# Pads that let the two operands of nearly all matrix products begin at one place modulo 512 bytes, and one shared temporary of the router

## The chip, the core and the metric

The kernel runs on one core of a Trainium2 chip. Its time is the device time of one execution in microseconds (us). The core's engines are TensorE (PE; its weight loads are a row of their own, PEld), VectorE (DVE), ScalarE (ACT), GpSimd (POOL) and SyncE (SP), which issues most DMAs. Each runs its own instructions in order and waits for others by semaphores.

## The reference: what is computed

Three layers follow each other: masked attention with decaying weights (4 sequences of 576 positions, 8 heads of 64), a dense mixture of 8 experts over the 2304 tokens, weighted by a matrix P that eight rounds of row and column normalisation make, and a mixture in which each token goes to one expert.

```python
# attention, per batch and head
ret = scale * (q @ k.T) * where(i >= j, gamma ** (i - j), 0);  x = ret @ v      # x: [2304, 512]
# dense mixture: E = 8, D = 512, F = 1024
P = exp(x @ w_gate - max);  8 times: rows of P to sum 1, columns of P to sum N / E
out = sum over e of P[:, e] * (relu(x @ w1[e]) @ w2[e])
# mixture with one expert per token
e = argmax(x @ w_gate);  out = softmax(x @ w_gate)[e] * (relu(x @ w1[e]) @ w2[e])
```

## The kernel before, in words

All products are done in a split form: an fp32 operand a is kept as a high part in the format fp32r and a low part (the rest), and a product becomes three matmuls: high by high, high by low, low by high. On TensorE a matmul is a weight load (the stationary operand, 128 columns of 4 bytes, so 512 bytes in each partition) and a matmul that streams the moving operand (512 columns, 2048 bytes, in most places) past it. A row `pyt<-w2hi,hhi` of the profile names the result, the moving operand and the stationary one, in that order.

The stages, in order of time:

- **Attention** (`attention`): 16 pairs of heads, in an order that a table of numbers (`TAU`) sets. Its matmuls are transposes (L160, 128 or 64 columns), scores (L209) and outputs (L273) of 256 or 128 columns, and small products of 128 columns (L235).
- **Dense mixture** (`Dense`), two sweeps of 16 units (half of an expert each). `hidden` makes the hidden rows of eight tiles of tokens by seven products of combined blocks, 84 matmuls of 512 columns in a unit (L608, in `product`): moving operands `op0h` to `op6l` of pool `xT`, stationary ones `w0h` to `w6l` of pool `b_w1`. `y_tile` (L730) multiplies 128 hidden rows by `w2hi`, `w2lo` in 12 matmuls of 512 columns; the hidden rows are stationary: `hhi`, `hlo` of pool `b_h`. In the first sweep two more tiles are made the plain way by `rest_hidden` (L705, 256 columns, moving `xrh`, `xrl`, stationary `w0h` to `w3l`), and their rows `rhi`, `rlo` of pool `b_r` are the stationary operands of 24 matmuls at L730. ACT and DVE split the next unit's weights beside it and evict the results.
- **Router** (`Router`): the choice of expert, beside the second sweep, in small DVE instructions.
- **Slots** (`Top1`): 22 slots of 128 tokens that share an expert were executed here. `hidden` (L1248, 24 matmuls of 512 columns, moving `op0h` to `op3l`, stationary `xth`, `xtl`), transposes (`th` L1260, `tx` L1227), `result` (L1276, 24 matmuls of 512 columns, moving `op4h` to `op6l` and `u7h`, `u7l`, stationary `hth`, `htl`). `split` (L1214 on ACT, L40 on DVE, or on POOL for the units 3 and 7) makes each expert's weights ready.

In ACT, DVE and PE the order of the code is the order of the instructions. In a slot, ACT has the queue hrow, hth, xth, hth, then the splits 0, 1, 3, 2 of the next slot, and then 4, 5; DVE has the low parts of the same.

A tile's place is fixed when the program is built: the tiles of a pool lie behind each other in the order in which they are made, each rounded up to 32 bytes, and a pool lies behind the one that was opened before it. The pools `b_h`, `b_q`, `b_w2`, `b_w1` and `xb` are laid from the other end (`side="right"`).

```python
for k in range(2):                                                    # product, around L608
    for ww, xx in ((wh, xh), (wl, xh), (wh, xl)):
        self.nc.tensor.matmul(bank, ww[:, k, 128 * p:128 * p + 128], xx[:, k, :], ...)
for hh, ww in ((hhi, vhi), (hhi, vlo), (hlo, vhi)):                   # y_tile, around L730
    nc.tensor.matmul(pt, hh, ww, start=n == 0, stop=n == 11)
mm = [(hi, fc, w[fc][i]) for fc in fcs for i in range(2)]             # result, around L1276
mm += [(lo, fc, w[fc][0]) for fc in fcs]
```

Of the kernel before, what the change touches and what calls it, by code (L numbers as in the profile page):

```python
# [10 lines left out]
F32 = mybir.dt.float32  # L11
# [12 lines left out]
E = 8  # L24
# [26 lines left out]
def attention(tc, ctx, q, k, v, gk, gq, ident, xseg, extra=(), npairs=16):  # L51
# [11 lines left out]
    const = ctx.enter_context(tc.tile_pool(name="a_const", bufs=1))  # L63
# [8 lines left out]
        return ENG[LO[k]]  # L72

    gk_sb = const.tile([128, H + 2 * NPAIR], F32, name="gk_sb")
    gq_sb = const.tile([128, NPAIR, 128], F32, name="gq_sb")
    kTs = [[const.tile([128, 640], F32R, name=f"kT{i}_{j}") for j in range(2)] for i in range(BUFS["kT"])]
    qbds = [[const.tile([128, 1152], F32R, name=f"qbd{i}_{j}") for j in range(2)] for i in range(BUFS["qbd"])]
# [307 lines left out]
class Pumped:  # L385


    def __init__(self, eng):
        self.eng, self.bg = eng, []
# [393 lines left out]
class Router:  # L783
# [8 lines left out]
    def __init__(self, tc, ctx, crow, ident, wg2, acc, x2d, res, pt):  # L792
        self.tc, self.nc, self.ident, self.acc, self.pt = tc, tc.nc, ident, acc, pt
        self.x2d, self.res = x2d, res
        nc = self.nc
        self.v = Pumped(nc.vector)
        self.pool = pool = ctx.enter_context(tc.tile_pool(name="r_sb", reuse_waits="tile", bufs=1))
        self.C = pool.tile([128, CKEEP], F32, name="crow")
        nc.scalar.dma_start(self.C, crow[:, 0:CKEEP])
        self.wg = pool.tile([128, KD, E], F32, name="wg2")  # L800
        nc.scalar.dma_start(self.wg, wg2.rearrange("(k p) e -> p k e", p=128))
        self.C16 = pool.tile([128, 3, 128], BF16, name="c16")
        with tc.tile_pool(name="r_c", reuse_waits="tile", bufs=1) as tmp:
            t = tmp.tile([128, 384], F32, name="crow_b")
            nc.scalar.dma_start(t, crow[:, CKEEP:CKEEP + 384])
            nc.vector.tensor_copy(self.C16.rearrange("p a b -> p (a b)"), t)
        self.L = pool.tile([128, NT, E], F32, name="L2")
        self.Bm = pool.tile([128, NT, 128], BF16, name="Bm")
        self.q = pool.tile([128, NT], F32, name="rq")
        self.gp = pool.tile([128, 3, NT], BF16, name="gparts")  # L810
        self.oh = [pool.tile([128, E, n], BF16, name=f"oh{n}") for n in (NEARLY, NLATE)]
        self.xt = pool.tile([128, KD, 128], F32, name="rxt")
        self.B = [{}, {}]

    def c(self, k):
# [17 lines left out]
    def choose(self, b, pool):  # L833

        nc, v = self.nc, self.v
        i0, n = ((0, NEARLY), (NEARLY, NLATE))[b]
        L = self.L[:, i0:i0 + n, :]
        m = pool.tile([128, n], F32, name=f"m{b}")
        eq = pool.tile([128, n, E], F32, name=f"eq{b}")
        mm = pool.tile([128, n], F32, name=f"mm{b}")  # L840
        w = self.c("w").unsqueeze(1).to_broadcast([128, n, E])
        v.tensor_reduce(out=m, in_=L, axis=AX.X, op=ALU.max)
        v.tensor_tensor(out=eq, in0=L, in1=m.unsqueeze(2).to_broadcast([128, n, E]), op=ALU.is_equal)
        v.tensor_tensor(out=eq, in0=eq, in1=w, op=ALU.mult)
        v.tensor_reduce(out=mm, in_=eq, axis=AX.X, op=ALU.max)
        v.tensor_tensor(
            out=self.oh[b].rearrange("p e i -> p i e"), in0=w,
            in1=mm.unsqueeze(2).to_broadcast([128, n, E]), op=ALU.is_equal,
        )
        self.B[b].update(m=m, i0=i0, n=n, pool=pool)  # L850

    def count(self, b):
        nc, r = self.nc, self.B[b]
# [116 lines left out]
    def early(self, pool):  # L970

        nc, v = self.nc, self.v
        n = NEARLY
        sel = pool.tile([128, E, n], F32, name="s0_sel")
        a = pool.tile([128, n], F32, name="s0_a")
        at = pool.tile([128, 2, n], F32, name="s0_at")
        z = pool.tile([128, n, 2, 2], BF16, name="s0_z")
        v.tensor_tensor(
            out=sel, in0=self.oh[0], in1=self.st.unsqueeze(2).to_broadcast([128, E, n]), op=ALU.mult
        )  # L980
        v.tensor_reduce(out=a, in_=sel.rearrange("p e i -> p i e"), axis=AX.X, op=ALU.add)
        for t in range(2):
            v.scalar_tensor_tensor(
                out=at[:, t, :], in0=self.q[:, 0:n], scalar=float(t), in1=a, op0=ALU.is_equal,
                op1=ALU.mult,
            )
        for t in range(2):
            v.tensor_scalar(
                out=z[:, :, 0, t], in0=at[:, t, :], scalar1=self.c("p"), scalar2=None, op0=ALU.mult
            )  # L990
            v.tensor_tensor(out=z[:, :, 1, t], in0=at[:, t, :], in1=self.c("i")[:, 0:n], op=ALU.mult)
        self.z0 = z
# [341 lines left out]
def build(ctx, tc, q, k, v, moe_w_gate, moe_w1, moe_w2, moe2_w_gate, moe2_w1, moe2_w2,  # L1334
          c_gk, c_gq, c_row, out):
    nc = tc.nc
    const = ctx.enter_context(tc.tile_pool(name="const", bufs=1))
    dram = ctx.enter_context(tc.tile_pool(name="dram", bufs=1, space=bass.MemoryType.DRAM))
    x2d = dram.tile([N, DM], F32, name="x2d")
    xbd = dram.tile([128, (NBLK - PB0) * KD * 64], F32, name="xbd")  # L1340
    ident = const.tile([128, 128], F32, name="ident")
    make_identity(nc, ident)
    res = {
        "gidx0": const.tile([128, 2], U32, name="gidx0"),
# [46 lines left out]
    with ExitStack() as cx:  # L1391
        lgp = cx.enter_context(tc.tile_pool(name="lgT", bufs=1, side="right"))
        xbp = cx.enter_context(tc.tile_pool(name="xb", bufs=1, side="right"))
        xb = xbp.tile([128, NBLK - PB0, KD, 64], F32, name="xb")

        def xseg(b, n):
            m = min(max(PB0 - b, 0), n)
            return ([(xa, b, m)] if m else []) + ([(xb, b + m - PB0, n - m)] if m < n else [])

        with ExitStack() as c2:  # L1400
            nc.scalar.dma_start(wg, moe_w_gate.rearrange("(k p) e -> p k e", p=128))
            p = nc.gpsimd
            tasks = token_tasks(nc, xa[:, 0:16], ops, [p, p, p, p, p, p, p])
            extra = [(4.0, lambda _: D.load1(0)), (5.0, lambda _: D.load2(0)),
                     (8.3, lambda ps: gate(ps, "ps", xa, 0, 4, 0)),
                     (8.5, lambda ps: gate(ps, "ps", xa, 4, 4, 8)),
                     (11.8, lambda ps: gate(ps, "ps", xa, 8, 2, 16))]
            extra += [(8.8 + 0.5 * i, lambda _, t=t: t()) for i, t in enumerate(tasks)]
            with tc.manual_schedule(engines={mybir.EngineType.SP}):
                attention(tc, c2, q, k, v, c_gk, c_gq, ident, xseg, extra)  # L1410
        aux = ctx.enter_context(tc.tile_pool(name="aux", reuse_waits="tile", bufs=1, space=PSUM))
        D.pt = aux
        for i in range(0, NT - NEARLY, 4):
            gate(aux, "rt", xb, NEARLY + i, 4, 2 * i)
        nc.sync.dma_start(xbd, xb.rearrange("p b k t -> p (b k t)"))
# [143 lines left out]
    with tc.manual_schedule(engines=MANUAL):  # L1559
# [58 lines left out]
    n = nc.values_load(  # L1618
        res["nslot"][0:1, 0:1], min_val=NFULL, max_val=NSLOT,
        skip_runtime_bounds_check_because="18 to 26 slots hold 2304 tokens of 8 experts",  # L1620
    )
# [40 lines left out]
```

## Time and profile before

| | |
|---|---|
| time of 3 runs: median (lowest to highest) | 2022.6 us (2021.27 to 2023.38) |
| time of the profiled execution | 2022.26 us |
| its span, from the first to the last instruction | 2020.5 us |
| busy: PE, PEld, DVE, ACT, POOL | 1981.2, 1630.0, 1251.7, 847.7, 298.6 us |

The profiled execution's time is 1.8 us over its span and 0.3 us under the median. Busy times are the union of an engine's instructions. The shown length of a matmul is modelled and overlaps the next one's, so the pace of TensorE is read from the starts of its matmuls and not from their lengths.

### The profile page before, as it was taken

How to read it: one execution, taken by the hardware profiler on the slowest of the kernel's cores; microseconds unless marked ns; L12 is line 12 of the kernel's file. 1: busy time of each engine (PE TensorE's matmuls, PEld its weight loads, DVE VectorE, ACT ScalarE, POOL GpSimd, SP SyncE). 2: the span in 40 equal slices, each digit the busy share in tenths (PEclk: the TensorE clock that was granted, in tenths of full speed). 3: DMA queues.
4: the chain of work that ended last, by engine and by line, in shares of the span. 5: the costliest groups of instructions: out<-in, count | busy, mean ns of one | idle time of the engine just before them, and what ended most of it. 6: DMA issues, size and time to landing. Idle time of an engine off the chain costs nothing.

```text
span 2020.5 us, 25446 instructions
## 1 busy us (share of the span) xinstructions
PE 1981.2 (98%) x9584; PEld 1630.0 (81%) x9584; DVE 1251.7 (62%) x2059; ACT 847.7 (42%) x1454; POOL 298.6 (15%) x250
## 2 busy tenths in 40 slices
PE   8989999999999999999999999999999999999997
PEld 7777888888888888888878888888878888777775
DVE  7897565555455555554454555555576654988886
ACT  6665424222222223322333333333333334577785
POOL 5572000000000000000000000000000001466654
PEclk9999999999999999999999999999999999999999
DMA  5521111111111110111301111111112113112755
GB/s 130 141 59 64 42 43 42 42 42 42 42 42 42 42 37 27 42 42 42 110 33 63 42 42 63 42 45 60 42 42 63 42 63 115 43 43 74 250 199 189
DMA packets 112111, 134.94 MB, mean 67 GB/s; under 512 B 62190, under 2 KB 62446, under 8 KB 111600
## 3 DMA queue, kind: packets, MB, share of 16 engines
q1 hardware_dynamic: 106960, 121.92, 18.7%
q0 software_dynamic: 3680, 11.02, 1.7%
q8 instruction: 77, 1.26, 0.2%
q10 hardware_dynamic: 1344, 0.33, 0.1%
q14 instruction: 50, 0.41, 0.1%
HBM read 182.53 MB, written 12.58 MB: 97 GB/s over the span
## 4 chain that ended last, share of the span: by engine, by line
PE 83%; DVE 8%; ACT 5%; issue 3%; POOL 1%; SPq 0%; ACTq 0%; DMA 0%; POOLq 0%; DVEq 0%
PE pyt L730 37%; PE pha L608 17%; PE phc L608 8%; PE phr L705 5%; PE phb L608 4%; PE phs L1248 4%; DVE op2l L40 2%; PE po L273 2%; PE ps L209 1%; PE pS L235 1%; ACT op3h L1214 1%; ACT op2h L1214 1%; PE pgate L1376 1%; PE rpl L830 1%; ACT op0h L1214 1%
## 5 line engine op out<-in xcount | busy, mean ns | idle before, releaser
L730 PE MATMUL pyt<-w2hi,hhi 128*128 128x512 f32 x1024 | 402.6, 393 | 2.2 <-DVE xb L741 2.1
L730 PE MATMUL pyt<-w2lo,hhi 128*128 128x512 f32 x1024 | 399.2, 390 | 0.0
L730 PE MATMUL pyt<-w2hi,hlo 128*128 128x512 f32 x1024 | 399.2, 390 | 0.0
L634 ACT ACTIVATE q<-pha 128x512 f32<-128x512 f32 x192 | 114.4, 597 | 273.8 <-PE pha L608 269.4
L622 ACT ACTIVATE hhi<-q 128x512 fp32r<-128x512 f32 x192 | 121.5, 633 | 252.9 <-DVE q L630 252.9
L730 PEld LDWEIGHTS pyt<-w2hi,hhi 128*128 128x128 f32 x1024 | 192.3, 188 | 42.8 <-DVE xb L741 2.6
L730 PEld LDWEIGHTS pyt<-w2hi,hlo 128*128 128x128 f32 x1024 | 192.3, 188 | 40.7
L730 PEld LDWEIGHTS pyt<-w2lo,hhi 128*128 128x128 f32 x1024 | 192.4, 188 | 39.1
L623 DVE SCALAR_TENSOR_TENSOR hlo<-q,hhi 128x512 fp32r<-128x512 f32 x192 | 133.0, 693 | 96.9 <-ACT hhi L622 90.9
L741 DVE SCALAR_TENSOR_TENSOR xa<-pyt,P,xa 128x512 f32<-128x512 f32 x140 | 105.0, 750 | 139.2 <-PE pyt L730 138.4
L630 DVE TENSOR_TENSOR q<-phb,q 128x512 f32<-128x512 f32 x64 | 44.3, 692 | 172.9 <-PE phb L608 172.9
L741 DVE SCALAR_TENSOR_TENSOR xb<-pyt,P,xb 128x512 f32<-128x512 f32 x120 | 90.1, 751 | 96.4 <-PE pyt L730 96.1
L630 DVE TENSOR_TENSOR q<-phc,q 128x512 f32<-128x512 f32 x128 | 87.7, 686 | 36.0 <-PE phc L608 35.0
L40 POOL TENSOR_TENSOR op2l<-xb,op2h 128x1024 fp32r<-128x1024 f32 x1 | 2.4, 2402 | 728.1 <-ACT op2h L493 728.1
L560 ACT ACTIVATE w3h<-raw 128x512 fp32r<-128x512 f32 x31 | 19.6, 632 | 164.1 <-DVE raw L566 164.1
L566 DVE TENSOR_TENSOR raw<-raw 128x512 f32<-128x512 f32 x124 | 85.1, 686 | 1.1
L40 DVE TENSOR_TENSOR w2lo<-raw,w2hi 128x512 fp32r<-128x512 f32 x124 | 84.6, 683 | 0.0
L713 DVE SCALAR_TENSOR_TENSOR rlo<-phr,rhi 128x512 fp32r<-128x512 f32 x32 | 22.1, 692 | 90.4 <-ACT rhi L712 90.4
L586 ACT ACTIVATE w2hi<-raw 128x512 fp32r<-128x512 f32 x124 | 77.1, 623 | 0.0
L906 POOL TENSOR_SCALAR Bm<-c,ro 128x128 bf16<-128x128 bf16 x2 | 1.3, 652 | 461.9 <-PE pyt L730 461.9
L560 ACT ACTIVATE w4h<-raw 128x512 fp32r<-128x512 f32 x31 | 19.6, 632 | 116.3 <-DVE raw L566 116.3
L40 DVE TENSOR_TENSOR op2l<-raw,op2h 128x1024 fp32r<-128x1024 f32 x22 | 60.8, 2763 | 10.1 <-ACT op2h L1214 9.6
(391 smaller groups left out, 4789.2 us busy)
## 6 DMA issues: line engine op xcount, KB each, us to landing
raw<-in_moe_w_dram SPq DMA_DIRECT2D x180, 512.0 KB
raw<-in_moe_w_dram SPq DMA_DIRECT2D x62, 1024.0 KB
kt<-in_k_dram SPq DMA_DIRECT2D x32, 128.0 KB
vt<-in_v_dram SPq DMA_DIRECT2D x32, 128.0 KB
qt<-in_q_dram SPq DMA_DIRECT2D x32, 128.0 KB
x2d<-xa SPq DMA_DIRECT2D x10, 256.0 KB
xbd<-xb SPq DMA_DIRECT2D x1, 2048.0 KB
xb<-xbd SPq DMA_DIRECT2D x2, 1024.0 KB
```

The costliest lines, as they stand in the source:

```text
L40: return eng.tensor_tensor(out=out, in0=src, in1=hi.bitcast(F32), op=ALU.subtract)
L566: nc.vector.tensor_tensor(out=q(*out), in0=q(*a), in1=q(*b), op=op)
L586: nc.scalar.activation(hi, self.raw2[:, fc, :], AF.Copy)
L608: self.nc.tensor.matmul(bank, ww[:, k, 128 * p:128 * p + 128], xx[:, k, :], start=start and n == 0, stop=stop and n == 5, skip_group_check ...
L622: nc.scalar.activation(hi, c, AF.Relu)
L623: nc.vector.scalar_tensor_tensor(out=lo, in0=c, scalar=0.0, in1=hi.bitcast(F32), op0=ALU.max, op1=ALU.subtract)
L630: self.nc.vector.tensor_tensor(out=s, in0=p, in1=s, op=ALU.add)
L634: self.nc.scalar.activation(t, c, AF.Copy)
L705: nc.tensor.matmul(pt[:, j, :], w[:, k, 128 * j:128 * j + 128], xr[x][:, xi, k, :], start=n == 0, stop=n == 11,)
L730: nc.tensor.matmul(pt, hh, ww, start=n == 0, stop=n == 11)
L741: nc.vector.scalar_tensor_tensor(out=acc, in0=pt, scalar=P[:, i, e:e + 1], in1=acc, op0=ALU.mult, op1=ALU.add)
L1248: nc.tensor.matmul(ph, xx[:, k, :], ww[:, fs], start=n == 0, stop=n == 11)
```

## The change

Four tiles that nothing writes or reads are added (`pad0` and `pad1` in `const`, `pad2` in `a_const`, `pad3` in `r_sb`), and what is allocated behind them moves up. The router's `sel` takes the memory of `eq`, which is not read any more at that point, instead of 320 bytes of its own.

```diff
@@ build, pool const
+    const.tile([128, 88], F32, name="pad0")
     ident = const.tile([128, 128], F32, name="ident")
+    const.tile([128, 8], F32, name="pad1")
     make_identity(nc, ident)
@@ attention, pool a_const
     gk_sb = const.tile([128, H + 2 * NPAIR], F32, name="gk_sb")
+    const.tile([128, 112], F32, name="pad2")
     gq_sb = const.tile([128, NPAIR, 128], F32, name="gq_sb")
@@ Router.__init__, pool r_sb
         self.xt = pool.tile([128, KD, 128], F32, name="rxt")
+        pool.tile([128, 8], F32, name="pad3")
@@ Router.choose
-        self.B[b].update(m=m, i0=i0, n=n, pool=pool)
+        self.B[b].update(m=m, eq=eq, i0=i0, n=n, pool=pool)
@@ Router.early
-        sel = pool.tile([128, E, n], F32, name="s0_sel")
+        sel = self.B[0]["eq"].rearrange("p i e -> p (i e)").rearrange("p (e i) -> p e i", e=E)
```

Where the tiles begin, in bytes modulo 512, as the two built programs have them (within a tile every matmul here takes whole steps of 512 bytes, so that each of its slices begins at the same place):

| matmuls | moving operand | before | after | stationary operand | before | after |
|---|---|---|---|---|---|---|
| L608, 512 columns | op0h to op6l | 96 | 480 | w0h to w6l | 480 | 480 |
| L730, of eight tiles | w2hi, w2lo | 480 | 480 | hhi, hlo | 480 | 480 |
| L730, of two tiles | w2hi, w2lo | 480 | 480 | rhi, rlo | 96 | 480 |
| L705, 256 columns | xrh, xrl | 96 | 480 | w0h to w3l | 480 | 480 |
| L1248 | op0h to op3l | 96 | 480 | xth, xtl | 384 | 480 |
| L1276, of units 4 to 6 | op4h to op6l | 96 | 480 | hth, htl | 384 | 480 |
| L1276, of unit 7 | u7h, u7l | 384 | 480 | hth, htl | 384 | 480 |
| L209, L273, 256 and 128 columns | qbd, s | 160 | 480 | kT, S, vhi, vlo | 160 | 480 |
| L160, L825, L1227, L1260, transposes | ident | 128 | 480 | kt, qt; xa; xg; hrow | 160; 96; 384; 384 | 480 |

The matmuls of the gates and of the router (L1376, L830, L857, L858, L998, L1111, L1140) keep operands at different places. On each engine the same instructions stand in the same order in both programs; two DVE instructions of `early` name `eq` in place of `s_sel`. Of the waits three semaphores of the first unit's weight splits are gone (the DVE split `w1l` doesn't wait for two DMA queues any more, `w4l` not for POOL); no wait is added.

## Rows read from the trace of the kernel before

**Rows 1.** The page, part 4: the chain that ended last, by line.
```profile
PE pyt L730 37%; PE pha L608 17%; PE phc L608 8%; PE phr L705 5%; PE phb L608 4%; PE phs L1248 4%; DVE op2l L40 2%; PE po L273 2%; PE ps L209 1%; PE pS L235 1%; ACT op3h L1214 1%; ACT op2h L1214 1%; PE pgate L1376 1%; PE rpl L830 1%; ACT op0h L1214 1%
```

**Rows 2.** Windows by stage (attention, dense sweeps, slots): stretch, its length, each engine's busy time.
```profile
0.00:173.50 173.50, 158.61 (x1067) 134.17 (x1067) 145.53 (x368) 111.13 (x273) 111.74 (x147) 0.97 0.42 100
173.50:1713.00 1539.50, 1535.68 (x7142) 1267.93 (x7142) 849.60 (x1363) 519.37 (x901) 16.82 (x17) 1.00 0.15 50
1713.00:2020.50 307.50, 286.93 (x1379) 227.94 (x1377) 256.58 (x329) 217.20 (x280) 170.03 (x86) 0.98 0.38 132
```

**Rows 3.** Waits of PE over the whole span: total us, times, longest us.
```profile
PE phs L1248 <- DVE op2l L40: 4.8, 19, 1.0
...
PE pyt L730 <- DVE xb L741: 2.1, 1, 2.1
...
PE pha L608 <- ACT q L634: 0.9, 1, 0.9
```

**Rows 4.** Groups of PE by line and operands: xcount, busy us, mean ns, idle before.
```profile
L730 PE MATMUL pyt<-w2hi,hhi 128*128 128x512 f32 x1024 | 402.6, 393 | 2.2 <-DVE xb L741 2.1
...
L608 PE MATMUL pha<-op0h,w0h 128*128 128x512 f32 x128 | 50.7, 396 | 0.0
...
L705 PE MATMUL phr<-xrh,w0h 128*128 128x256 f32 x64 | 18.1, 283 | 0.0
...
L1248 PE MATMUL phs<-op1h,xth 128*128 128x512 f32 x44 | 17.5, 398 | 0.0
```

**Rows 5.** Timeline of PE, one unit of the first sweep: start us, length us, instruction.
```profile
572.30 0.40 PE L730 MATMUL pyt<-w2hi,rhi 128*128 128x512 f32 x1
...
577.89 0.40 PE L730 MATMUL pyt<-w2hi,hhi 128*128 128x512 f32 x1
...
599.69 0.40 PE L608 MATMUL pha<-op0h,w0h 128*128 128x512 f32 x1
...
610.88 0.28 PE L705 MATMUL phr<-xrh,w0h 128*128 128x256 f32 x1
...
613.73 0.39 PE L608 MATMUL phc<-op3h,w3h 128*128 128x512 f32 x1
```

**Rows 6.** Timeline of PE, hidden rows of a unit of the second sweep.
```profile
1365.54 0.40 PE L608 MATMUL pha<-op0h,w0h 128*128 128x512 f32 x1
...
1385.13 0.39 PE L730 MATMUL pyt<-w2hi,hhi 128*128 128x512 f32 x1
```

**Rows 7.** Timeline of PE in attention, outputs of 256 columns.
```profile
161.02 0.28 PE L273 MATMUL po<-s,vhi 128*128 128x256 f32 x1
...
161.38 0.52 PE L273 MATMUL po<-qbd,S 128*128 128x256 f32 x3
```

**Rows 8.** Timeline of PE in one slot.
```profile
1839.30 0.50 PE L1248 MATMUL phs<-op2l,xth 128*128 128x512 f32 x1 [0.21 <-DVE op2l L40]
...
1848.53 0.40 PE L1276 MATMUL pys<-u7h,hth 128*128 128x512 f32 x1
...
1849.44 0.63 PE L1276 MATMUL pys<-op6h,htl 128*128 128x512 f32 x2
1849.91 0.62 PE L1276 MATMUL pys<-u7h,htl 128*128 128x512 f32 x2
1850.37 0.40 PE L1248 MATMUL phs<-op0h,xth 128*128 128x512 f32 x1
```

**Rows 9.** Timeline of ACT in that slot.
```profile
1843.57 0.60 ACT L1253 ACTIVATE hrow<-phs 128x512 f32<-128x512 f32 x1 [0.25 <-PE phs L1248]
...
1848.34 1.08 ACT L1214 ACTIVATE op2h<-raw 128x1024 fp32r<-128x1024 f32 x1
```

**Rows 10.** Timeline of DVE in that slot.
```profile
1847.75 1.22 DVE L40 TENSOR_TENSOR op1l<-raw,op1h 128x1024 fp32r<-128x1024 f32 x1
1849.44 2.88 DVE L40 TENSOR_TENSOR op2l<-raw,op2h 128x1024 fp32r<-128x1024 f32 x1 [0.47 <-ACT op2h L1214]
```

**Rows 11.** Timeline of POOL in that slot.
```profile
1848.56 2.68 POOL L40 TENSOR_TENSOR op3l<-raw,op3h 128x1024 fp32r<-128x1024 f32 x1 [1.47 <-ACT op3h L1214]
```

## The prediction

> **What bounds the kernel now.** I read the page first, then a table of busy time by stage, the waits of PE, and PE's timeline, since the change does nothing but move tiles to other addresses. In the chain of work that ended last, the lines of matmuls carry most of the span: L730 alone 37%, the three L608 groups 29% [rows 1]. The stages tell why: in the dense sweeps PE is busy 1535.7 of 1539.5 us, while DVE needs 849.6 and ACT 519.4 [rows 2]. What PE waits there is one 2.1 us wait for DVE, one of 0.9 us for ACT and crumbs [rows 3]. So in this stage each nanosecond off a matmul is a nanosecond off the span. In the slots PE is busy 286.9 of 307.5 us and DVE 256.6 [rows 2], and PE waits 19 times for the low part `op2l`, once for nearly each slot [rows 3]: another chain closes there, and a faster PE is not simply a faster slot.
>
> **The pace of matmuls at equal and at different places.** A busy PE says nothing of its pace; the starts do. The trace of before holds the experiment already, since some pairs of operands begin at one place modulo 512 and others don't. In one unit of the first sweep [rows 5]:
> - L730 on the eight tiles (both at 480): from 577.89 to 599.69, 96 matmuls in 21.80 us, 227.1 ns each.
> - L730 on the two other tiles (480 and 96), the same line with the same moving operands: from 572.30 to 577.89, 24 in 5.59 us, 232.9 ns.
> - L608 (96 and 480): from 599.69 to 610.88, 48 in 11.19 us, 233.1 ns.
> - In the second sweep a unit's whole `hidden`: 84 matmuls from 1365.54 to 1385.13, 19.59 us, 233.2 ns [rows 6].
>
> In a slot, `u7h` and `hth` (both at 384) go at 227.5 ns (1848.53 to 1849.44, four), or at 230 with `htl` (1849.91 to 1850.37, two), but `op6h` and `htl` (96 and 384) at 235 (1849.44 to 1849.91, two) [rows 8]. So the same code with the same shapes runs some 6 ns slower wherever the two places differ, with three different differences (128, 288 and 384). In the sweeps the weight loads are busy 1267.9 us of the same 1539.5 in which the matmuls are busy 1535.7 [rows 2], so a load runs beside the matmul ahead of it and both operands are read at once. That they get into each other's way is my inference; the 6 ns are the rows'.
>
> **The change part by part.**
>
> *L608.* The group of [rows 4] stands for 21 of its size, 128 each: 2688 matmuls. Both operands come to 480, the place of the fast L730. The gap is 233.1 - 227.1 = 6.0 ns; I take 5.8, since now and then an interval at equal places is longer too (the 230 above). 2688 x 5.8 = 15.6 us. Bounds: 3.1 ns, if the aligned pace is the 230 (8.3 us), and 6.1 ns (16.4 us).
>
> *L730 of the two tiles.* 24 in each of 16 units, 384: 232.9 - 227.1 = 5.8 ns, 2.2 us. These two are on PE's path nearly everywhere [rows 2, 3]: 17.8 us together.
>
> *L705, 256 columns.* It goes at 118.8 ns (24 in 2.85 us [rows 5]) with its operands apart, and the aligned matmuls of 256 columns in attention go at 120 (three from 161.02 to 161.38 [rows 7]). So here the place seems not to matter: 0 is what I take, nearest to this row. There are 12 groups of 64, 768 matmuls [rows 4]. Bounds: a gain in the proportion of L608 (2.6%, 3.1 ns) would give 2.4 us, and 120 a loss of 0.9 us.
>
> *The slots.* 22 slots of 24 matmuls at L1248 (the group of [rows 4] is one of 12, 528) and 18 of 24 at L1276 (unit 7 is at equal places already), 924 in all. If PE set the slot's time, that were 924 x 5.8 = 5.4 us. But follow a slot: DVE's `op2l` releases the row at 1839.30 [rows 8]; 17 matmuls later ACT takes the hidden row at 1843.57, goes without a pause through seven more instructions and ends `op2h` at 1849.42 [rows 9]; the next `op2l` takes 2.88 us more, to 1852.32 [rows 10], and releases the next slot. This loop of 13.07 us holds 17 of the slot's 48 matmuls, and the first of them is bound by its wait; the others wait with PE at `op2l`. So 16 x 19 = 304 matmuls count: at 3 to 5.8 ns 0.9 to 1.8 us, and I take 1.4. The first slots, where the loop hasn't closed yet, have 4 x 42 = 168 more, 1.0 us if all were on the path; between the router's waits I take 0.4.
>
> *Other operands.* ACT, DVE, POOL and the DMAs read and write at the new places too, and the trace has their operations only at the old ones. In the dense sweeps their idle time covers it [rows 2]. Without that cover there is only the slots' loop: 5.85 us of ACT and 2.88 of DVE [rows 9, 10], where 1% in either direction is 0.09 x 19 = 1.7 us. I take 0. Transposes of 128 columns, gates and scores I leave as they are.
>
> *The shared temporary, the pads, the waits.* `sel` in the place of `eq` is the same two small DVE instructions; the last reader of `eq` is an earlier instruction of DVE, so nothing new is waited for. Pads have no instruction. The three waits that go are in the first unit's weight splits; no wait of PE in [rows 3] comes from there, so they give 0.
>
> Sum: 15.6 + 2.2 + 1.4 + 0.4 = 19.6 us. The profiled execution took 2022.26 us (span 2020.5), 0.3 under the median of the three runs; 2022.26 - 19.6 = 2002.7 us.
>
> [...] By the rows, equal places are worth 5.8 ns a matmul, 19.6 us in all. [...]
>
> **The rivals.**
> 1. *The place is not what paces them.* L608, the two tiles and the slots would be slower for what their tiles are (made by other engines, other buffers, other steps), and pads change nothing: 2022.3 us. For it: no row shows the same tile at two places. Against it: L730 differs in nothing but the stationary tile, and three kinds of matmul at different places agree within some 2 ns. Chance 0.04.
> 2. *Half of it comes.* The pace at equal places is 230 ns for these too, as for `u7h` with `htl` [rows 8], because 480 is only one condition among several: 3072 x 3.1 = 9.5 us and 1.0 in the slots, 2011.8 us. Against it: 96 matmuls in a row hold 227.1 [rows 5]. Chance 0.08.
> 3. *More comes.* The slots' loop gives way (ACT and DVE a little faster at the new places) and PE sets the slots, 3.6 us more than the 1.8 of the loop, and L705 gains its 2.4: about 2002.7 - 6 = 1996.7 us. Against it: the 19 waits [rows 3] and the 120 ns [rows 7]. Chance 0.05.
> 4. *Slower: a second split of DVE collides with POOL's.* `op1l` takes 1.22 us, while `op2l`, the same operation on the same shape, takes 2.88 [rows 10]: POOL's `op3l` runs beside it from 1848.56 [rows 11]. [...] If the new times within the slot brought another of DVE's splits beside a POOL split, each slot would take 1.66 us more, 19 x 1.66 = 31.5 us against 19.6 gained: 2034 us. It decides from 19.6 / 19 = 1.03 us a slot. Against it: ACT's order spaces them, `op1l` keeps its 1.22 us although `op3l` begins 0.4 us before its end, and a slot's matmuls shift by 0.1 us only. Chance 0.03.
>
> **How the numbers follow.** The forecast has 0.80: 2002.7 us, its own range some 1999 to 2006 (the slots from 0 to 5.4 us, L705 from -0.9 to 2.4, ACT and DVE 1.7 either way). To 2010 the larger part of the second rival is in, to 1998 half of the third; 0.12 or so is left out. Faster by over 0.2%, which is about what these measurements can tell from no change (4 us): forecast and rivals 2 and 3, 0.93. Within 0.2%: rival 1, 0.04. Slower: rival 4, 0.03.
>
> **What would show it.** Starts of L608 and of the two tiles at L730 some 227 ns apart, L705 still at 118 to 120; the dense sweeps shorter by about 18 us (1539.5 to about 1522) with PE's waits there as they were; in the slots a loop of still about 13.0 us, and PE's waits for `op2l` up from 4.8 to some 7 us, since what PE saves outside the 17 matmuls goes there. The prediction is wrong if L608 stays over 232 ns, if the slots shorten by 4 us or more, or if `op1l` or `op0l` grows over 2 us.

## The result, and the profile after

The changed kernel took 2002.8 us (median of 5 runs, 2001.8 to 2006.32), the kernel before 2023.38 us beside it (5 runs, 2021.27 to 2025.12): a ratio of 0.9901, with a 95% interval of 0.9886 to 0.9915. The profiled execution took 2002.13 us with a span of 2000.3. Forecast were 2002.7 us and a range of 1998 to 2010. That the median stands 0.1 us from the forecast is partly luck: single executions of the changed kernel differ by up to 4.5 us; the forecast starts from an execution 1.1 us under the median of before measured here, and its gain of 19.6 us is 1.0 us under the 20.6 of the two medians.

After the change `product` is L609, `rest_hidden` L706, `y_tile` L731, and the slots' two matmul lines are L1250 and L1278. The first view is the table of windows by stage, as in [rows 2], cut at the first `pha` of the dense sweeps and the last `pyt`.

```profile
0.00:172.70 172.70, 157.54 (x1066) 132.31 (x1066) 146.08 (x368) 111.02 (x273) 112.05 (x147) 0.98 0.43 100
172.70:1694.30 1521.60, 1517.10 (x7142) 1267.41 (x7142) 849.38 (x1363) 519.11 (x901) 16.82 (x17) 1.00 0.15 51
1694.30:2000.30 306.00, 282.28 (x1378) 227.67 (x1376) 256.63 (x329) 217.58 (x280) 170.07 (x86) 0.98 0.38 132
```

Compared with [rows 2], the dense sweeps went from 1539.5 to 1521.6 us and the slots from 307.5 to 306.0, while the work of DVE, ACT and POOL in both is the same within 0.4 us. Taken at the starts of the same matmuls, the gains are 18.0 us in the dense sweeps, 1.4 in the slots and 0.8 in attention, together the 20.2 us by which the span shrank. Attention's 0.8 isn't shown to be the pads': in the six kernels below with the same code for attention the sweeps begin between 172.6 and 174.2 us, in the three without pads between 173.5 and 173.9.

The timeline of PE in one unit of the first sweep, as in [rows 5]: start, shown length, instruction.

```profile
566.95 0.39 PE L731 MATMUL pyt<-w2hi,rhi 128*128 128x512 f32 x1
...
572.39 0.39 PE L731 MATMUL pyt<-w2hi,hhi 128*128 128x512 f32 x1
...
594.15 0.39 PE L609 MATMUL pha<-op0h,w0h 128*128 128x512 f32 x1
...
605.03 0.28 PE L706 MATMUL phr<-xrh,w0h 128*128 128x256 f32 x1
...
607.90 0.40 PE L609 MATMUL phc<-op3h,w3h 128*128 128x512 f32 x1
```

The two tiles take 24 matmuls in 5.44 us, the eight tiles 96 in 21.76, L609 48 in 10.88: all three 226.7 ns apart. The 256-column L706 takes 24 in 2.87 us, 119.6 ns, where it had 118.8. Over all intervals under 250 ns between two matmuls of one kind the means went from 233.1 to 227.0 ns (L609, 2613 of them, 15.7 us), from 233.1 to 226.7 (two tiles, 2.4 us), from 227.3 to 227.1 (eight tiles, 2962 of them, 0.8 us) and from 119.4 to 119.7 (L706, -0.2 us). These add up to more than the 18.0 us of the sweeps, because the few longer intervals, the waits among them, took some 1.4 us more.

The hidden rows of a unit in the second sweep, as in [rows 6]:

```profile
1350.85 0.39 PE L609 MATMUL pha<-op0h,w0h 128*128 128x512 f32 x1
...
1369.89 0.39 PE L731 MATMUL pyt<-w2hi,hhi 128*128 128x512 f32 x1
```

84 matmuls in 19.04 us, 226.7 ns each, where there were 233.2. What PE waits for, over the whole span, as in [rows 3]:

```profile
PE phs L1250 <- DVE op2l L40: 7.5, 19, 1.2
...
PE pyt L731 <- DVE xb L742: 2.2, 1, 2.2
...
PE pha L609 <- ACT q L635: 1.1, 1, 1.1
```

In the dense sweeps the listed waits are nearly as they were (0.1 and 0.2 us longer). In the slots the 19 waits for `op2l` have grown from 4.8 to 7.5 us: PE comes earlier to a low part that comes hardly any earlier. A slot's edge in PE's timeline, as in [rows 8], shows the wait itself:

```profile
1830.19 0.62 PE L1278 MATMUL pys<-op6h,htl 128*128 128x512 f32 x2
1830.64 0.62 PE L1278 MATMUL pys<-u7h,htl 128*128 128x512 f32 x2
1831.09 0.39 PE L1250 MATMUL phs<-op0h,xth 128*128 128x512 f32 x1
...
1832.45 0.39 PE L1250 MATMUL phs<-op2h,xth 128*128 128x512 f32 x1
1833.17 0.50 PE L1250 MATMUL phs<-op2l,xth 128*128 128x512 f32 x1 [0.33 <-DVE op2l L40]
1833.51 0.39 PE L1250 MATMUL phs<-op2h,xtl 128*128 128x512 f32 x1
```

The `op6h` pair now takes 0.45 us, like the `u7h` pair (0.47 and 0.46 in [rows 8]). At `op2l` the starts stand 0.72 and then 0.34 us apart, where two matmuls without a wait stand 0.45 us apart in all: this wait costs 0.61 us, though the row lists 0.33, since a listed wait is counted from the modelled end of the matmul ahead of it. Over all 19 waits the starts give 12.7 us (10.1 before) where 7.5 are listed. The mean slot went from 13.14 to 13.07 us.

### The profile page after: what moved, and what is told of

Read it like the earlier page. It is cut to its first block, busy times and chain, and to the rows that moved or that the text cites. A ratio compares the mean times of both kernels' runs of the same rounds, so it can differ in the third digit from the quotient of the medians.

```text
span 2000.3 us, 25444 instructions
## 1 busy us (share of the span) xinstructions
PE 1956.9 (98%) x9584; PEld 1627.4 (81%) x9584; DVE 1252.1 (63%) x2059; ACT 847.7 (42%) x1454; POOL 298.9 (15%) x250
## 4 chain that ended last, share of the span: by engine, by line
PE 82%; DVE 8%; ACT 5%; issue 3%; DMA 1%; POOL 0%; SPq 0%; ACTq 0%; POOLq 0%; DVEq 0%
PE pyt L731 37%; PE pha L609 17%; PE phc L609 8%; PE phr L706 5%; PE phb L609 4%; PE phs L1250 4%; DVE op2l L40 2%; PE po L274 2%; PE ps L210 1%; ACT op3h L1216 1%; PE pS L236 1%; ACT op2h L1216 1%; PE rpl L832 1%; DMA raw<-in_moe_w_dram 1%; PE pgate L1381 1%
## 5 line engine op out<-in xcount | busy, mean ns | idle before, releaser
L731 PE MATMUL pyt<-w2hi,hhi 128*128 128x512 f32 x1024 | 402.5, 393 | 2.4 <-DVE xb L742 2.2
L731 PE MATMUL pyt<-w2hi,hlo 128*128 128x512 f32 x1024 | 398.9, 390 | 0.0
L731 PE MATMUL pyt<-w2lo,hhi 128*128 128x512 f32 x1024 | 398.5, 389 | 0.0
L731 PEld LDWEIGHTS pyt<-w2hi,hhi 128*128 128x128 f32 x1024 | 192.3, 188 | 42.8 <-DVE xb L742 2.9
L731 PEld LDWEIGHTS pyt<-w2hi,hlo 128*128 128x128 f32 x1024 | 192.2, 188 | 40.7
L731 PEld LDWEIGHTS pyt<-w2lo,hhi 128*128 128x128 f32 x1024 | 192.4, 188 | 38.8
L561 ACT ACTIVATE w3h<-raw 128x512 fp32r<-128x512 f32 x31 | 19.6, 631 | 160.4 <-DVE raw L567 160.3
L561 ACT ACTIVATE w4h<-raw 128x512 fp32r<-128x512 f32 x31 | 19.6, 632 | 116.2 <-DVE raw L567 116.2
L40 DVE TENSOR_TENSOR op2l<-raw,op2h 128x1024 fp32r<-128x1024 f32 x22 | 60.6, 2756 | 10.1 <-ACT op2h L1216 9.6
```

What stands on the lines that cost most here:

```text
L40: return eng.tensor_tensor(out=out, in0=src, in1=hi.bitcast(F32), op=ALU.subtract)
```

## The experiments

The theory was the prediction's: a 512-column matmul runs at its fast pace where its moving and its stationary operand begin at one place modulo 512 bytes. Its rivals were that the new place itself (480) matters, that some distances are harmless and others not, and, for the size of the gain, that the slots or the shared temporary hold more of it than thought. The last runs test the loop that holds the slots. A kernel with one run has no interval, and what it shows is read from its trace; the kernel before had medians of 2024.08 (first four below), 2024.17 (`at_448`, `unit3_dve`) and 2024.45 us (`all_256`, `unit3_no_pads`) on the same chips.

**Seven distances in one kernel.** `pad0` and `pad1` are taken out, and the seven pairs of blocks get steps between them, so that the moving operands of L609 stand 384, 352, 256, 192, 64, 32 and 0 bytes (`op0` to `op6`) from the stationary ones.

```diff
-    const.tile([128, 88], F32, name="pad0")
-    const.tile([128, 8], F32, name="pad1")
-    ops = [tuple(xpool.tile(...) for x in "hl") for o in range(7)]
+    for o, step in enumerate((0, 8, 24, 16, 32, 8, 8)):
+        if step:
+            xpool.tile([128, step], F32, name=f"step{o}")
+        ops.append(tuple(xpool.tile(...) for x in "hl"))
```

> The changed kernel without its first two pads; instead small pads inside the pool xT, so that the moving operands op0 to op6 stand at seven distances from their stationary operands: 384, 352, 256, 192, 64, 32 and 0 bytes modulo 512 (in this order). The tiles behind that pool are where the change has them. Theory 1 (only equal places modulo 512 are fast): the matmuls of op6 start 227 ns apart, those of the six others 232 to 235, whatever the distance; the two tiles of L731 stay at 227. Theory 2 (the modulus is 256 or less): op2 at distance 256 is at 227 as well, and by a modulus of 64 also op0, op3 and op4. Theory 3 (the whole step of the change was something else than the place): all seven alike. By theory 1 the time is about 2002.8 + 6/7 of 15.6 + 1.4, some 2017 us.

Measured: 2018.67 us (one run; some 2017 expected), span 2016.9. The timeline of PE through one unit's hidden rows in the second sweep:

```profile
1361.67 0.40 PE L609 MATMUL pha<-op0h,w0h 128*128 128x512 f32 x1
...
1364.46 0.40 PE L609 MATMUL phb<-op1h,w1h 128*128 128x512 f32 x1
...
1365.86 0.39 PE L609 MATMUL pha<-op4h,w4h 128*128 128x512 f32 x1
...
1368.65 0.39 PE L609 MATMUL phb<-op1h,w1h 128*128 128x512 f32 x1
...
1370.06 0.39 PE L609 MATMUL pha<-op5h,w5h 128*128 128x512 f32 x1
...
1372.86 0.39 PE L609 MATMUL phc<-op3h,w3h 128*128 128x512 f32 x1
...
1375.61 0.39 PE L609 MATMUL pha<-op6h,w2h 128*128 128x512 f32 x1
...
1376.99 0.39 PE L609 MATMUL pha<-op6h,w2h 128*128 128x512 f32 x1
...
1378.35 0.39 PE L609 MATMUL phc<-op2h,w6h 128*128 128x512 f32 x1
...
1381.07 0.39 PE L731 MATMUL pyt<-w2hi,hhi 128*128 128x512 f32 x1
```

From row to row: 384 bytes apart, 12 in 2.79 us (232.5 ns); 352, 6 in 1.40 (233); 64, 12 in 2.79 (232.5); 32, 12 in 2.80 (233); 192, 12 in 2.75 (229). At 0 the first six take 1.38 us (230 ns) and the next six 1.36 (227); at 256, 12 take 2.72 (226.7). Equal places modulo 512 are thus not the rule: 256 apart is as fast, and behind a series of slow matmuls the first ones at equal places are not at full pace yet. The distance of 192 costs less than the others: in the first sweep 233.5 ns where after has 229.0 for the same matmuls (they begin behind L706), in the second 229.1 where after has 226.7. The sweeps took 1535.6 us, 4.0 less than before (with a loss in them that is estimated at 1.6 after another profile in the last section).

**Which matmul pays.** Of the two tiles' stationary parts, `rlo` alone is moved 128 bytes off, so that in each step of three matmuls (`rhi`, `rhi`, `rlo`) one has an unequal stationary operand of its own, and the one ahead of it runs while that operand is loaded (before, a load of 0.19 us starts at 572.54, beside the matmul that starts at 572.53 and ahead of its own at 572.76).

```diff
@@ Dense.__init__
+        self.off = [1, 1]
@@ Dense.rest_hidden
+        if self.off[g]:
+            hp.tile([128, 32], F32, name=f"offa{g}")
         lo = hp.tile([128, 2, 256], F32R, name="rlo", tag=f"rlo{g}")
+        if self.off[g]:
+            hp.tile([128, 96], F32, name=f"offb{g}")
+            self.off[g] = 0
```

> The changed kernel with pads in pool b_r, so that the low rows rlo (stationary operands at L731 on the two tiles) stand 128 bytes from the others, and rhi stays at the place of the moving operands. The three matmuls of a step there are (rhi, w2hi), (rhi, w2lo), (rlo, w2hi), the stationary operand first. Theory 1a (a matmul is slowed by the place of the weights that are loaded beside it, those of the next matmul): the second, w2lo with rhi, goes from 227 to about 233 ns until the next start, the first and the third stay at 227. Theory 1b (slowed by its own stationary operand's place): the third, w2hi with rlo, goes to 233, the second stays. Either way 128 matmuls at 6 ns, 0.8 us, less than one look can tell in the time: 2002.8 to 2004.

Measured: 2006.22 us (one run), over the 2002.8 to 2004 that were expected; span 2004.4, of which some 1.6 us are put down to a fallen clock, an estimate after another profile in the last section. PE's timeline in the first sweep:

```profile
568.72 0.39 PE L737 MATMUL pyt<-w2hi,rhi 128*128 128x512 f32 x1
568.94 0.40 PE L737 MATMUL pyt<-w2lo,rhi 128*128 128x512 f32 x1
569.18 0.40 PE L737 MATMUL pyt<-w2hi,rlo 128*128 128x512 f32 x1
569.41 0.39 PE L737 MATMUL pyt<-w2hi,rhi 128*128 128x512 f32 x1
```

A step takes 0.69 us where it took 0.68. Over the trace (128 of each place in the step) the time to the next start is 226.7 ns where both this stationary operand and the next are equal, 232.5 where the next is unequal, and 234.2 where its own is. Both pay, where each of the two theories expected one, so a picture in which only the load of the next weights disturbs the stream is too small.

**The slots' pad alone taken out.** `pad3` goes, and `xth`, `xtl` and `hth`, `htl` stand 32 bytes from the moving operands; the dense sweeps keep their places.

```diff
-        pool.tile([128, 8], F32, name="pad3")
```

> The changed kernel without pad3: the slots' stationary operands xth, xtl, hth, htl stand 32 bytes from the moving operands op0 to op6 again, unit 7 stays equal, the dense sweeps stay as in the change. Theory 1 with the slots' own loop as the bound: matmuls of L1248 and of units 4 to 6 at L1276 at 232 to 235 ns, the dense sweeps at 227, and the time 1.2 to 1.8 us over the change's (2004.0 to 2004.6), with PE's waits for op2l back from 7.5 to about 5 us. Rival (PE sets the slots' time): 5.4 us over it, 2008.

Measured: 2005.7 us (median of 4, 2004.12 to 2006.7; 2004.0 to 2004.6 expected), a ratio to before of 0.9902 (0.9886 to 0.9919). That is the ratio of after, so the times can't tell 1.5 us; the stages of the profiles can. The slots by the window of their stage, and PE's wait:

```profile
1696.80:2004.30 307.50, 286.98 (x1378) 227.60 (x1376) 256.68 (x329) 217.63 (x280) 170.47 (x86) 0.98 0.39 132
```

```profile
PE phs L1249 <- DVE op2l L40: 4.8, 19, 1.0
```

307.5 us, as in [rows 2], against 306.0 after: `pad3` is worth 1.5 us. It is so in every profile with the loop in place: 305.9 to 306.1 us in the four where the slots' operands agree (after, `rlo`, 448, 256), 307.3 to 307.5 in the four where they don't. PE is busy 4.7 us longer, and PE's waits for `op2l` are back at 4.8 us: most of what the matmuls lose is taken from the wait. The other 1.9 us by which the dense sweeps of this profile are longer than those of after (1523.5 against 1521.6) are for the most part a fallen clock, told at the end.

**The shared temporary alone**, without the pads:

```diff
-        self.B[b].update(m=m, i0=i0, n=n, pool=pool)
+        self.B[b].update(m=m, eq=eq, i0=i0, n=n, pool=pool)
...
-        sel = pool.tile([128, E, n], F32, name="s0_sel")
+        sel = self.B[0]["eq"].rearrange("p i e -> p (i e)").rearrange("p (e i) -> p e i", e=E)
```

> The kernel before with the shared temporary alone, no pad. It moves the slots' tiles by 320 bytes down, to another distance from their moving operands, and nothing in the dense sweeps. Theory 1: the same time as before, 2022 to 2023.5 us, L608 at 233 ns. Rival (the shared temporary gives part of the gain): over 1 us faster than before.

Measured: 2023.62 us (median of 10), ratio 0.9995 (0.9985 to 1.0005). The interval leaves room for 3 us of gain; the stages of the profiles leave less, 1539.5 and 307.4 us as before. By itself it is worth nothing that can be seen, so the gain comes with the pads. In the change its 320 bytes are still part of what places the slots' tiles: the 416 bytes of `pad0`, `pad1` and `pad3` alone would take `xth` and `hth` from 384 to 288 modulo 512, and the 320 taken off bring them to 480.

**Another common place.** `pad0` is 8 floats shorter and the pools of the other end get a pad of 8 floats: all that stood at 480 stands at 448.

```diff
-    const.tile([128, 88], F32, name="pad0")
+    const.tile([128, 80], F32, name="pad0")
+    right = ctx.enter_context(tc.tile_pool(name="right", bufs=1, side="right"))
+    right.tile([128, 8], F32, name="padr")
```

> The changed kernel with all tiles of both ends moved by 32 bytes: pad0 is 32 bytes smaller, and a pool at the right end takes 32 bytes, so that the operands of L609, L731, L1250, L1278 begin at 448 modulo 512 in place of 480, again all at one place. Theory 1 (equality counts, not which place): the change's time, 2002 to 2004 us, and 227 ns at L609 and L731. Rival (480, 32 bytes ahead of a boundary of 512, is a good place of its own): L609 and L731 both slower than 228 ns, by up to 6 ns on some 5800 matmuls, up to 35 us.

Measured: 2005.65 us (median of 4, 2003.58 to 2008.16), over the 2002 to 2004 expected; the ratio of 0.9912 (0.9896 to 0.9927) overlaps that of after. L609 has a mean of 227.1 ns, and the profile has a fallen clock in its sweeps (0.74 from 1475 to 1480 us). The place 480 is not what matters.

**All dense operands 256 bytes apart.** `pad0` is 24 floats: what is laid from the left stands at 224, what is laid from the right at 480. The slots' operands stay equal.

```diff
-    const.tile([128, 88], F32, name="pad0")
+    const.tile([128, 24], F32, name="pad0")
```

> The changed kernel with pad0 256 bytes smaller: all that lies at the left end begins at 224 modulo 512, what lies at the right end stays at 480. The dense sweeps' operands at L609, at L706 and of the two tiles at L731 are then 256 bytes apart modulo 512, and equal modulo 256; the slots' operands are all equal (224). Theory A, as predicted (places have to be equal modulo 512): L609 at 233 ns, 17.8 us slower than the change, about 2020.6 us. Theory B (modulo 256 is enough, as the group at distance 256 in the run with seven distances suggests, which however came behind a settled row of equal ones): 227 ns at L609 from the first products of a unit on, and the change's time, 2001 to 2006 us.

Measured: 2003.32 us (median of 4, 2001.97 to 2003.5), ratio 0.9892 (0.9876 to 0.9909). PE's timeline through a unit's hidden rows:

```profile
1352.36 0.39 PE L609 MATMUL pha<-op0h,w0h 128*128 128x512 f32 x1
...
1371.40 0.39 PE L731 MATMUL pyt<-w2hi,hhi 128*128 128x512 f32 x1
```

84 matmuls in 19.04 us, 226.7 ns, at a distance of 256 throughout. In these runs the same place modulo 256 bytes is enough (226.7 ns at a distance of 256, as at 0), and by the distances of 64, 128 and 192, which are slow (232.5, 232.5 to 234.2 and 229 ns), no smaller step is.

**The slots' loop cut.** After, with the low part of unit 3 made by DVE and not by POOL, so that no POOL instruction runs beside DVE's `op2l`.

```diff
-            eng = self.nc.gpsimd if c in (3, 7) else self.nc.vector
+            eng = self.nc.gpsimd if c == 7 else self.nc.vector
```

> The changed kernel with one edit: the low part of unit 3 of each slot's weights (op3l) is made by DVE and not by POOL. Theory (the slots are bound by the loop from the hidden row over ACT's splits and op2l, in which op2l takes 2.88 us since POOL's op3l runs beside it): op2l falls to about 1.22 us, DVE has op3l of 1.22 us ahead of it and still ends about 0.9 us earlier; PE's waits for op2l (7.5 us in all) mostly go, and the time falls by 5 to 7.5 us, to 1995.5 to 1998 us. Rival (PE's own pace already sets the slots, the waits are covered): the same time as the change, or slower, as DVE has more to do in a slot.

Measured: 1989.21 us (median of 5, 1988.59 to 1993.45), ratio 0.9834 (0.9821 to 0.9848), which beats both kernels. DVE's timeline in a slot:

```profile
1850.10 1.22 DVE L40 TENSOR_TENSOR op3l<-raw,op3h 128x1024 fp32r<-128x1024 f32 x1
1851.23 1.22 DVE L40 TENSOR_TENSOR op2l<-raw,op2h 128x1024 fp32r<-128x1024 f32 x1
1852.37 0.74 DVE L1325 TENSOR_SCALAR o<-pys,gate 128x512 f32<-128x512 f32 x1
```

Two splits now take 2.35 us on DVE, from 1850.10 to 1852.45, where `op2l` alone took 2.88 [rows 10], and no wait of PE for `op2l` is listed. The slots fall to 291.9 us:

```profile
1695.50:1987.40 291.90, 276.59 (x1378) 229.09 (x1376) 242.40 (x350) 217.31 (x280) 114.21 (x65) 0.98 0.40 139
```

That is 14.1 us less than after and more than was expected. A slot takes 12.37 us and not 13.07, 18 x 0.70 = 12.6, and the part behind the last slot's begin is 1.4 shorter. The expectation went by the listed waits, 7.5 us; by the starts the 19 waits cost 12.7. The 1.4 us that is left isn't traced to an instruction.

**The same cut without the pads**, to see what they are worth where PE sets the slots too: the kernel before with that one line.

> The kernel before, without pads, with unit 3's low part made by DVE. With the slots' loop gone PE's pace sets the slots in both versions, so the pads should be worth more than the 20.6 us of the change: 17.8 in the dense sweeps and 42 matmuls at 5 to 6 ns in each of some 19 to 22 slots, 4.0 to 5.5 us, so 22 to 23.3 us above the 1989.2 us of the version with pads and the same edit: 2011 to 2012.5 us. Rival (the slots stay bound by another engine, so that places count there as little as before): 17.8 + 1.4, 2008.4 us.

Measured: 2012.86 us (median of 4; 2011 to 2012.5 expected), ratio 0.9942 (0.9925 to 0.9959). The slots:

```profile
1714.60:2011.40 296.80, 281.78 (x1378) 229.29 (x1376) 242.69 (x350) 217.23 (x280) 128.32 (x65) 0.99 0.39 136
```

With and without pads the two kernels lie 23.65 us apart (on two chips, with 2024.45 and 2024.17 us for the kernel before). In the profiles the sweeps differ by 19.5 us (1541.0 against 1521.5; before has 1539.5 with the same code in them, and the 1.5 us between the two are put down to a fallen clock, of which the last section tells), and the slots by 4.9 (296.8 against 291.9), of which 18 x (12.61 - 12.37) = 4.3 us are the slots' pace; with the loop in place the slots gained 1.4. That pace fits PE as the bound: 42 matmuls at 5.9 ns are 0.25 us a slot.

## Why the prediction was right, point by point

- **Where PE sets the end, pace is time.** Right: the sweeps gained 18.0 us where L608's and the two tiles' terms were 15.6 + 2.2, and PE's listed waits there grew by 0.3 us only [rows 3]. The prediction's first two rivals (the place doesn't matter; half of it comes) fall with 226.7 ns on the lines that had 233, and the first of them also with `rlo` apart: 226.7 against 232.5 and 234.2 ns, changed by nothing but 128 bytes of the stationary operand's address.
- **5.8 ns a matmul.** Right in size, a little low: 6.0 and 6.4 in the means. The reserve was taken off because equal pairs sometimes go at 230. The traces show where they do. Before, the eight tiles follow the slow two tiles, and their first eight matmuls are 231 ns apart; after, they follow fast ones and are at 226 to 227 from the first:

```profile
577.89 0.40 PE L730 MATMUL pyt<-w2hi,hhi 128*128 128x512 f32 x1
...
579.74 0.39 PE L730 MATMUL pyt<-w2hi,hlo 128*128 128x512 f32 x1
```

```profile
572.39 0.39 PE L731 MATMUL pyt<-w2hi,hhi 128*128 128x512 f32 x1
...
574.20 0.39 PE L731 MATMUL pyt<-w2hi,hlo 128*128 128x512 f32 x1
```

  That is the most of the eight tiles' 0.8 us, which the sum didn't have. The `u7h` pair at 230 [rows 8], from which the second rival took its price, stood behind a slow pair too.
- **L705 at nothing.** Right; at 119.6 ns it is within the bound of 120, a loss of 0.2 us.
- **The slots.** 1.4 us, where 1.4 for the loop and 0.4 for the first slots were forecast; they gave 1.1 and 0.2. The mean slot stands at 13.07 us, from 13.14, where a loop of still about 13.0 was forecast; the waits for `op2l` were to grow to some 7 us and are 7.5. Taking `pad3` out takes the 1.5 us back, and with the loop cut the pads are worth 4.9 there, so it is shown that a loop that ends in `op2l` bounds the slots. Its way from PE through ACT's splits is read from [rows 9] and wasn't cut by itself.
- **The third and fourth rivals.** The slots' loop didn't give way. No second split collided: DVE's busy time in the slots is 256.6 us in both, where a collision in each slot would have added over 30. That `op2l` is slow because of POOL's split beside it is shown by moving that split: 1.22 us and not 2.88. Why the one slows the other, no run here tells.
- **What fell of the theory.** "One place modulo 512" was more than is needed here; modulo 256 does it (226.7 ns at 256). And the inference that the next weights' load disturbs the stream is half of it: the matmul whose own stationary operand is unequal is slow as well (234.2 ns, and 232.5 for the one ahead of it). What holds a matmul up, and why it takes some seven or eight matmuls to come back to full pace, no run here tells.

## What to carry to other kernels

Compare the start-to-start pace of matmuls of one shape over different operand tiles: where some run a few per cent slower, look at where their two operands begin, and pad them to one place modulo 256 bytes (here 233 to 227 ns at 512 columns with an fp32r weight load for each matmul; at 256 columns nothing, for the one distance that L706 tried). It paid where PE sets the end (18.0 us in the sweeps), so find the loop that closes elsewhere first: one line that moved a POOL split to DVE gave another 13.6 us, and made the pads in the slots worth three times as much (4.9 us, not 1.5). Price a short wait from starts (12.7 us here), not from the idle time that is listed for it (7.5).

## What the runs showed of the hardware

- Distances of 32, 64, 128, 352 and 384 bytes between the two operands cost some 6 to 8 ns of 227 for each 512-column matmul, 192 bytes 2 to 5; 0 and 256 cost nothing in a long series (all at 226.7 to 227.1).
- Equal pairs behind a slow series start some 231 ns apart for seven or eight matmuls and then 227 (the eight tiles before, `op6` in the seven distances). Behind L706, the equal pairs of L609 do so after too: 232 ns for the first five.
- Without `pad3` and at 448 the granted clock falls behind PE's wait of 2.2 us for the router's `xb`, to 0.53 for 3.4 us in the first, and to 0.74 from 1475 to 1480 us and 0.92 to 1485 in the second. PE's timeline without `pad3`:

```profile
1476.95 0.50 PE L731 MATMUL pyt<-w2hi,hhi 128*128 128x512 f32 x1 [2.21 <-DVE xb L742]
...
1478.03 0.63 PE L731 MATMUL pyt<-w2lo,hhi 128*128 128x512 f32 x1
1478.46 0.63 PE L731 MATMUL pyt<-w2hi,hlo 128*128 128x512 f32 x1
```

and the windows around them (the granted clock is the third column from the end):

```profile
1472.00:1477.70 5.70, 3.49 (x15) 2.57 (x15) 5.39 (x22) 0.63 (x1) 1.30 (x2) 1.00 0.00 0
1477.70:1481.10 3.40, 3.40 (x10) 2.59 (x10) 1.67 (x8) 0.00 (x0) 0.00 (x0) 0.53 0.77 205
```

The clock is 0.53 there, and eight matmuls start some 0.42 us apart and not 0.23: 1.6 us of the 1.9 that this profile's sweeps are longer. The profiles of after and before have the same wait, 2.2 and 2.1 us, and 0.23 us from start to start behind it, at a clock of 1.00; with unit 3 on DVE the clock stays at 1.00 behind 2.2 us too. For the seven distances and `rlo` the 1.6 us is an estimate after the profile without `pad3`; for unit 3 without pads it is the 1.5 us by which its sweeps are longer than those of before. So two profiles of one stage can differ by that much though PE's wait ahead of it is the same; what decides whether the clock falls, these runs don't tell.
